# A softplus written with a biased logarithm, and the last weight splits moved from GpSimd to VectorE

## The chip, the cores and the metric

The program runs on one core of one Trainium2 chip. A core has a matrix engine (TensorE, PE in the profile; its weight loads are shown apart as PEld), VectorE (DVE), ScalarE (ACT), GpSimd (POOL) and a queue engine that issues DMAs (SyncE, SP). The metric is the device time of one execution in microseconds (us), as a median over runs.

## The reference, cut to what matters

```python
x = attention(q, k, v)                     # 1152 rows of 512
x = mixture_of_experts(x, ...)             # top 2 of 8 experts, weights w1, w2
h = x @ w_in                               # 1152 x 2048
g = np.maximum(h, 0.0) + np.log1p(np.exp(-np.abs(h)))
return (g @ w_out).astype(np.float32)      # 1152 x 512
```

The change touches only the last three lines, the feed-forward part: the function g (softplus) and the preparation of its weights. Everything is float32 and is kept close to float32 accuracy: each operand of a product is split into a high part in a rounded format and a low part (operand minus high part), and each product is made of three matmuls, high by high, high by low and low by high.

## The kernel before, in words

Attention and routing fill the first part of the span, the experts the middle, and the feed-forward part runs from about 459 us to the end. There the 1152 rows lie in four groups of 2, 3, 2 and 2 tiles of 128 rows (`CH`), and the 2048 hidden columns in 16 blocks of 128. A step n handles one group and one block: 64 steps, n = 0 to 63, and three more in which only the rest of the second product is left. The first 16 steps belong to group 0, with 256 columns in an instruction.

In step n the program issues, in this order: `act2(n-1)` on VectorE; at some steps a part of the next rows' combination (`scale0` on ScalarE and `combine` on VectorE at steps 3, 7, 11, ...; a transpose on TensorE with its two copies, tiles `xh` and `xl`, at steps 6, 10, 14, ..., and behind it two gathers, `ygather`, on GpSimd); `ff1_(n)`, the first product, 12 matmuls into the PSUM tile `ph`, then Abs and Exp on ScalarE; `act3(n-1)`, the high part `gh` of the softplus on ScalarE; `act1(n)`; the low part `gl` of step n-1 on VectorE; `split_lo`; `split_hi`; and `ff2_(n-3)`, the second product of the step three before, six matmuls for a group of two tiles, of which the third and the sixth read `gl`.

The weights come as 80 chunks of 128 by 1024 numbers, in four buffers `wraw`. `split_hi` makes a chunk's high part on ScalarE; the low part is put in a list and done by the next `split_lo` as one subtraction, behind which the load of the chunk four further on is issued by SP. The engine of that subtraction is picked once per chunk in line 169. When the feed-forward part begins, chunks 71 to 79 are still to be split, nine in all; `split_hi` takes them at steps 0 to 8, so that their low parts come at steps 1 to 9.

Each engine works its instructions strictly in the order in which the program issues them, and waits for data of other engines by semaphores. No scheduler orders this part.

Of the kernel before, what the change touches and what calls it, by code (L numbers as in the profile page):

```python
# [16 lines left out]
AF = mybir.ActivationFunctionType  # L17
OP = mybir.AluOpType
# [34 lines left out]
NWA, NWB, NWC = 6, 5, 5  # L53
# [50 lines left out]
def fused_kernel(ctx: ExitStack, tc: tile.TileContext, q, k, v, w_gate, w_noise, noise, w1, w2,  # L104
                 w_in, w_out, cs_t, out):
    nc = tc.nc
# [35 lines left out]
    pools = {}  # L142
    nxt = {"load": 0, "split": 0, "order": False}

    def load_chunk():
        s = nxt["load"]
        if s >= len(chunk_src) or s >= 8 and not nxt["order"]:
            return
        nxt["load"] += 1
        t = raw.tile([128, 1024], F32, name="wraw")  # L150
        src = chunk_src[s]() if s < 8 * E else chunk_src[s]
        nc.sync.dma_start(out=t.rearrange("p (a b) -> p a b", a=4 if s < 8 * E and s % 8 < 4 else 2), in_=src)
        chunk_raw[s] = t
# [3 lines left out]
    def wtile(i):  # L157
        return (wa if i < NWA else pools["wb"]).tile([128, 2048], F32R, name=f"w{i}")

    def split_hi():  # L160
        s = nxt["split"]
        nxt["split"] += 1
        if s >= 64 + NSLOT:
            w = pools["wc"].tile([128, 2, 1024], F32R, name="wc")
        else:
            w = wtile(s % NSLOT).rearrange("p (a b) -> p a b", a=2)
        hi, lo = w[:, 0], w[:, 1]
        r = chunk_raw.pop(s)
        lo_eng = nc.gpsimd if s < NWA or "wc" in pools else nc.vector
        nc.scalar.activation(hi, r, AF.Copy)  # L170
        chunk[s] = (hi, lo)

        def second():
            lo_eng.tensor_tensor(out=lo, in0=r, in1=hi.bitcast(F32), op=OP.subtract)  # L174
            load_chunk()
        lo_q.append(second)

    def split_lo():
        while lo_q:
            lo_q.pop(0)()  # L180

    def split_chunk():
        split_hi()
        split_lo()
# [52 lines left out]
    def win_blk(kk, f):  # L237
        h, l = chunk[64 + 2 * (f // 2)]
        o = kk * 256 + (f % 2) * 128
        return h[:, o:o + 128], l[:, o:o + 128]  # L240
# [6 lines left out]
    def mm3(ps, pairs, first, last):  # L247
        n = len(pairs)
        for i, ((ah, al), (bh, bl)) in enumerate(pairs):
            nc.tensor.matmul(ps, ah, bh, start=first and i == 0, stop=False)  # L250
            nc.tensor.matmul(ps, ah, bl, start=False, stop=False)  # L251
            nc.tensor.matmul(ps, al, bh, start=False, stop=last and i == n - 1)  # L252
# [710 lines left out]
    for g in range(2 * NP_):  # L963
        p, h = divmod(g, 2)
        for u in range(6):
            n = 5 * g + (0, 1, 2, 3, 3, 4)[u]
# [6 lines left out]
        for a in range(2):  # L973
            n = 5 * g + 3 + a
# [3 lines left out]
        n = 5 * g + 5  # L978
# [4 lines left out]
    for p in range(NP_):  # L983
        n = 10 * p
# [54 lines left out]
    for i in range(NWA):  # L1039
        op(("sp", i), "ACT", 950, 100 + i, [("ld", i) if i < 4 else ("sl", i - 4), ("rope", 7)] + [("sp", i - 1)] * (i > 0) +  # L1040
           prep7 * (i >= 4) + [("XTl", 0), ("XTl", 1)] * (i == 5), split_hi)
        op(("sl", i), "POOL", 2300, 100, [("sp", i)], lambda: lo_q.pop(0)())
# [101 lines left out]
    for _ in range(8):  # L1144
        next(r1)
    split_hi()
    for f in range(4, 8):
        gemm1(0, f, pa)
# [191 lines left out]
    def ygather(i, kk):  # L1340
        nonlocal ygt
        if ygt is None:
            ygt = yg_tile().bitcast(F32)
        o = (i % 3 if kk == 0 else 3 + i % 2) * DM
        g = ygt[:, o:o + DM]
        top = (NOV + ROW0[NR - 1] + (min(i + 1, CB) if kk else 0)) * 128
        nc.gpsimd.indirect_dma_start(out=g, out_offset=None, in_=ytab[0:top, :],
                                     in_offset=bass.IndirectOffsetOnAxis(ap=yrow[:, i, kk:kk + 1], axis=0))
        YG[i, kk] = g
# [4 lines left out]
    def scale0(i):  # L1354
        a = YG[i, 0]
        nc.scalar.activation(a, a, AF.Copy, scale=wts[:, i, 0:1])

    def combine(i):
        a, c = YG.pop((i, 0)), YG.pop((i, 1))
        nc.vector.scalar_tensor_tensor(out=c, in0=c, scalar=wts[:, i, 1:2], in1=a, op0=OP.mult, op1=OP.add)  # L1360
        YG[i] = c

    def x2_T(i, ps):
        y = YG.pop(i)
        for d in range(4):
            nc.tensor.transpose(ps[:, d, :], y[:, d * 128:(d + 1) * 128], ident)
        c, o = place[i]
        if o == 0:
            x2[c] = (mx.tile([128, 4, FC], F32R, name="xh"), mx.tile([128, 4, FC], F32R, name="xl"))
        dh, dl = (t[:, :, o * 128:(o + 1) * 128] for t in x2[c])  # L1370
        nc.scalar.activation(dh, ps, AF.Copy)
        nc.vector.tensor_tensor(out=dl, in0=ps, in1=dh.bitcast(F32), op=OP.subtract)  # L1372
# [45 lines left out]
    def ff1_(c, f):  # L1418
        w = CH[c] * 128
        ps = psh.tile([128, FC], F32, name="ph")[:, :w]  # L1420
        xh, xl = x2[c]
        mm3(ps, [(win_blk(kk, f), (xh[:, kk, :w], xl[:, kk, :w])) for kk in range(4)], True, True)
        a = ff.tile([128, FC], F32, name="fa")[:, :w]
        l = ff.tile([128, FC], F32, name="fl")[:, :w]
        u = ff.tile([128, FC], F32, name="fu")[:, :w]
        HS[c, f] = (ps, a, l, u)
        nc.scalar.activation(a, ps, AF.Abs)  # L1427
        nc.scalar.activation(a, a, AF.Exp, scale=-1.0)  # L1428

    def act1(c, f):  # L1430
        ps, a, l, u = HS[c, f]
        nc.vector.tensor_scalar(u, a, 1.0, None, op0=OP.add)  # L1432
        nc.vector.scalar_tensor_tensor(out=a, in0=u, scalar=1.0, in1=a, op0=OP.subtract, op1=OP.subtract)
        return lambda: nc.scalar.activation(l, u, AF.Ln)

    def act2(c, f):
        ps, a, l, u = HS[c, f]
        nc.vector.scalar_tensor_tensor(out=l, in0=ps, scalar=0.0, in1=l, op0=OP.max, op1=OP.add)
        nc.vector.tensor_tensor(out=l, in0=l, in1=a, op=OP.subtract)

    def act3(c, f):
        ps, a, l, u = HS.pop((c, f))
        gh = ff.tile([128, FC], F32R, name="gh", bufs=FL + 1)[:, :CH[c] * 128]
        gl = ff.tile([128, FC], F32R, name="gl", bufs=FL + 1)[:, :CH[c] * 128]
        nc.scalar.activation(gh, l, AF.Copy)
        G[c, f] = (gh, gl)
        return lambda: nc.vector.tensor_tensor(out=gl, in0=l, in1=gh.bitcast(F32), op=OP.subtract)

    def ff2_(c, f, o):
        gh, gl = G[c, f]  # L1450
        if f == 0:
            ACC[c, o] = pso.tile([128, DM], F32, name="po")
        cs = slice(o * 128, o * 128 + 128)
        mm3(ACC[c, o], [((gh[:, cs], gl[:, cs]), wout_blk(f))], f == 0, f == 15)
        if f == 15:
            i = place.index((c, o))
            po = ACC.pop((c, o))
            ot = ff.tile([128, DM], F32, name="ot", bufs=2)
            if i == NT - 1:
                nc.scalar.activation(ot[:, 0:DM // 2], po[:, 0:DM // 2], AF.Copy)  # L1460
                nc.vector.tensor_copy(out=ot[:, DM // 2:], in_=po[:, DM // 2:])
            elif o % 2:
                nc.scalar.activation(ot, po, AF.Copy)
            else:
                nc.vector.tensor_copy(out=ot, in_=po)
            for t, r0, nr, p0, p1, base in tok_maps:
                if t <= i < t + nr:
                    nc.sync.dma_start(out=ap(out, (base + i - t) * DM, [[nr * DM, p1 - p0], [1, DM]]),
                                      in_=ot[p0:p1, :])
# [6 lines left out]
    seq = [(c, f) for c in range(len(CH)) for f in range(16)]  # L1476
# [7 lines left out]
    for n in range(len(seq) + FL):  # L1484
        if 1 <= n <= len(seq):
            act2(*seq[n - 1])
        for i, u in extra.pop(n, []):
            if u == 0:
                scale0(i)
                combine(i)  # L1490
            else:
                x2_T(i, psh.tile([128, 4, 128], F32, name="px", bufs=1))
                if i + 2 < NT:
                    ygather(i + 2, 0)
                    ygather(i + 2, 1)
        if n < len(seq):
            ff1_(*seq[n])
        sub = act3(*seq[n - 1]) if 1 <= n <= len(seq) else None
        if n < len(seq):
            act1(*seq[n])()  # L1500
        if sub:
            sub()
        split_lo()
        if nxt["split"] < len(chunk_src):
            split_hi()
        if n >= FL:
            c, f = seq[n - FL]
            for o in range(CH[c]):
                ff2_(c, f, o)
# [38 lines left out]
```

## Time and the profile before

| what | us |
|---|---|
| median of 3 runs (lowest, highest) | 684.37 (683.69, 684.41) |
| profiled execution, its own time | 683.52 |
| its span, first to last instruction | 681.7 |
| busy in the span: PE, PEld | 633.8, 566.9 |
| busy in the span: DVE, ACT, POOL | 515.1, 430.9, 249.3 |

The span is what the trace shows; the 1.8 us between it and the execution's own time lie around the program. The clock that TensorE was granted is full in all 40 slices of the page.

### The profile page before, as it was taken

Reading aid. Unit: us, or ns where it says so; the run is one execution under the profiler, and the core shown is the slowest. Engines: PE = TensorE matmul, PEld = TensorE weight load, DVE = VectorE, ACT = ScalarE, POOL = GpSimd, SP = SyncE. Lnnn points to the kernel's source line nnn. Section 1 sums busy time; section 2 is a strip of 40 time slices with the busy share of each in tenths; the row PEclk is TensorE's granted clock in tenths of the full one; section 3 lists DMA queues with packets and bytes.
Section 4 is the critical chain, followed back from the end, with each engine's and each line's share of the span. In section 5 each row is a group of like instructions: output and inputs, shape, how many; then the busy total and the mean of one; then the engine's idle time right before and its main releaser. Section 6 shows DMA issues by size and latency. Waiting matters only on the chain.

```text
span 681.7 us, 11588 instructions
## 1 busy us (share of the span) xinstructions
PE 633.8 (93%) x4066; PEld 566.9 (83%) x4066; DVE 515.1 (76%) x1054; ACT 430.9 (63%) x912; POOL 249.3 (37%) x250
## 2 busy tenths in 40 slices
PE   2899999889988999999999999977799999999997
PEld 2798989868987898988889798956579999899996
DVE  6889899999985658849686776837997655676665
ACT  2887888668973656747576576726565544465553
POOL 6968976762465202432323232316650100000000
PEclk9999999999999999999999999999999999999999
DMA  6318421002342959997999999764311100100000
GB/s 152 95 42 308 134 56 55 1 19 76 120 129 85 341 161 302 345 319 275 327 311 329 313 314 340 245 233 137 96 53 43 45 17 0 46 2 1 32 1 31
DMA packets 67900, 101.07 MB, mean 148 GB/s; under 512 B 11232, under 2 KB 38624, under 8 KB 67840
## 3 DMA queue, kind: packets, MB, share of 16 engines
q1 hardware_dynamic: 61552, 84.59, 38.2%
q0 software_dynamic: 3136, 10.10, 4.5%
q10 hardware_dynamic: 3152, 5.62, 2.2%
q8 instruction: 33, 0.54, 0.3%
q14 instruction: 27, 0.22, 0.1%
HBM read 76.70 MB, written 23.59 MB: 147 GB/s over the span
## 4 chain that ended last, share of the span: by engine, by line
PE 57%; DVE 4%; ACT 4%; DMA 2%; issue 0%; ACTq 0%; DVEq 0%; SPq 0%
PE p L250 9%; PE p L251 9%; PE p L252 9%; PE po L252 4%; PE po L251 4%; PE po L250 4%; PE ph L250 4%; PE ph L252 4%; PE ph L251 4%; DVE fu L1432 2%; DMA wraw<-wtab 2%; PE p L1117 2%; PE pa L1073 1%; PE p L1119 1%; DVE yg L1360 1%; ACT wc L170 1%
## 5 line engine op out<-in xcount | busy, mean ns | idle before, releaser
L219 POOL TENSOR_TENSOR dm<-dm,da 128x512 int32<-128x512 int32 x32 | 42.1, 1314 | 134.1 <-DVE da L216 61.2
L174 DVE TENSOR_TENSOR w<-wraw,w 128x1024 fp32r<-128x1024 f32 x65 | 88.6, 1374 | 1.2 <-ACT w L170 1.2
L170 ACT ACTIVATE w<-wraw 128x1024 fp32r<-128x1024 f32 x75 | 78.7, 1055 | 8.7 <-DMA wraw<-in_moe_w_dram 7.9
L251 PE MATMUL p<-xl,w 128*128 128x320 f32 (+3 forms) x256 | 77.4, 303 | 0.3 <-DVE xl L1076 0.3
L250 PE MATMUL p<-xh,w 128*128 128x320 f32 (+3 forms) x256 | 77.4, 303 | 0.0
L252 PE MATMUL p<-xh,w 128*128 128x320 f32 (+3 forms) x256 | 77.3, 302 | 0.0
L1432 DVE TENSOR_SCALAR fu<-fa 128x256 f32<-128x256 f32 (+1 forms) x64 | 31.5, 492 | 56.5 <-ACT fa L1428 56.5
L1427 ACT ACTIVATE fa<-ph 128x256 f32<-128x256 f32 (+1 forms) x64 | 26.1, 407 | 68.1 <-PE ph L252 68.1
L483 ACT ACTIVATE P<-ps,nmx 128x576 f32<-128x576 f32 (+1 forms) x80 | 59.2, 740 | 12.8 <-DVE nmx L475 11.7
L475 DVE TENSOR_REDUCE nmx<-ps 128x1 f32<-128x576 f32 (+1 forms) x80 | 60.0, 751 | 7.4 <-PE ps L462 5.6
L518 ACT ACTIVATE pth<-pt 128x512 fp32r<-128x512 f32 (+2 forms) x96 | 53.4, 569 | 9.2 <-PE pt L496 4.9
L250 PE MATMUL p<-w,hb 128*128 128x512 f32 x144 | 58.7, 407 | 0.0
L250 PE MATMUL ph<-xh,w 128*128 128x256 f32 (+1 forms) x192 | 57.2, 298 | 1.4 <-DVE xl L1372 1.4
L1093 DVE SCALAR_TENSOR_TENSOR hb<-p,hb 128x256 fp32r<-128x256 f32 (+1 forms) x104 | 31.6, 346 | 34.0 <-ACT hb L1089 32.4
L252 PE MATMUL ph<-xh,w 128*128 128x256 f32 (+1 forms) x192 | 56.7, 295 | 0.0
L251 PE MATMUL ph<-xl,w 128*128 128x256 f32 (+1 forms) x192 | 56.7, 295 | 0.0
L252 PE MATMUL p<-w,hb 128*128 128x512 f32 x144 | 56.6, 393 | 0.0
L251 PE MATMUL p<-w,hb 128*128 128x512 f32 x144 | 56.6, 393 | 0.0
L448 DVE TENSOR_TENSOR ptl<-pt,pth 128x512 fp32r<-128x512 f32 (+1 forms) x80 | 49.5, 629 | 1.7 <-ACT pth L518 1.2
L251 PEld LDWEIGHTS p<-xl,w 128*128 128x128 f32 x256 | 48.2, 188 | 0.8 <-DVE xl L1076 0.5
L250 PEld LDWEIGHTS p<-xh,w 128*128 128x128 f32 x256 | 48.2, 188 | 0.7 <-ACT xh L1075 0.2
L252 PEld LDWEIGHTS p<-xh,w 128*128 128x128 f32 x256 | 48.2, 188 | 0.0
(291 smaller groups left out, 1882.2 us busy)
## 6 DMA issues: line engine op xcount, KB each, us to landing
wraw<-in_moe_w_dram SPq DMA_DIRECT2D x64, 512.0 KB
x<-in_moe_w_in_dram SPq DMA_DIRECT2D x16, 512.0 KB
x<-in_moe_w_out_dram SPq DMA_DIRECT2D x16, 512.0 KB
wtab<-dm SPq DMA_DIRECT2D x32, 256.0 KB
wraw<-wtab SPq DMA_DIRECT2D x16, 512.0 KB
ytab<-y ACTq DMA_DIRECT2D x18, 256.0 KB
ytab<-zrow SPq DMA_DIRECT2D x1, 4096.0 KB
w<-in_v_dram SPq DMA_DIRECT2D x8, 256.0 KB
```

Source lines behind the costliest of these rows:

```text
L170: nc.scalar.activation(hi, r, AF.Copy)
L174: lo_eng.tensor_tensor(out=lo, in0=r, in1=hi.bitcast(F32), op=OP.subtract)
L219: nc.gpsimd.tensor_tensor(out=m, in0=m, in1=ai, op=OP.add)
L250: nc.tensor.matmul(ps, ah, bh, start=first and i == 0, stop=False)
L251: nc.tensor.matmul(ps, ah, bl, start=False, stop=False)
L252: nc.tensor.matmul(ps, al, bh, start=False, stop=last and i == n - 1)
L448: nc.vector.tensor_tensor(out=dl, in0=x, in1=dh.bitcast(F32), op=OP.subtract)
L475: nc.vector.tensor_reduce(out=nmx[p0:p1], in_=stS[n][p0:p1, :, :HN], axis=AX.XY, op=OP.max, negate=True)
L483: nc.scalar.activation(Pt[p0:p1, 0:S].rearrange("p (a c) -> p a c", a=2), ps[p0:p1, :, :HN], AF.Exp, bias=nmx[p0:p1], scale=1.0, accum_out ...
L518: nc.scalar.activation(*evac.pop(("T", g, u)), AF.Copy)
L1093: nc.vector.scalar_tensor_tensor(out=o, in0=ps[:, c], scalar=0.0, in1=hh[:, c].bitcast(F32), op0=OP.max, op1=OP.subtract)
L1432: nc.vector.tensor_scalar(u, a, 1.0, None, op0=OP.add)
```

## The change

Three edits, all in the feed-forward part. The logarithm log(1 + a), with a = Exp(-|h|), is taken on ScalarE from a with a bias of one, directly behind the Exp, where before VectorE made u = 1 + a and ScalarE took the logarithm of u. VectorE makes the rounding correction from u = (1 + a) - 1 as a - u, with a two-operation instruction and a subtraction, where before it was (u - 1) - a; `act2` adds it now. And the low parts of the last nine chunks, 71 to 79, are made by VectorE.

```diff
         r = chunk_raw.pop(s)
-        lo_eng = nc.gpsimd if s < NWA or "wc" in pools else nc.vector
+        lo_eng = nc.gpsimd if s < NWA else nc.vector
         nc.scalar.activation(hi, r, AF.Copy)
...
         nc.scalar.activation(a, ps, AF.Abs)
         nc.scalar.activation(a, a, AF.Exp, scale=-1.0)
+        nc.scalar.activation(l, a, AF.Ln, bias=1.0)
 
     def act1(c, f):
+
         ps, a, l, u = HS[c, f]
-        nc.vector.tensor_scalar(u, a, 1.0, None, op0=OP.add)
-        nc.vector.scalar_tensor_tensor(out=a, in0=u, scalar=1.0, in1=a, op0=OP.subtract, op1=OP.subtract)
-        return lambda: nc.scalar.activation(l, u, AF.Ln)
+        nc.vector.tensor_scalar(u, a, 1.0, 1.0, op0=OP.add, op1=OP.subtract)
+        nc.vector.tensor_tensor(out=a, in0=a, in1=u, op=OP.subtract)
 
     def act2(c, f):
         ps, a, l, u = HS[c, f]
         nc.vector.scalar_tensor_tensor(out=l, in0=ps, scalar=0.0, in1=l, op0=OP.max, op1=OP.add)
-        nc.vector.tensor_tensor(out=l, in0=l, in1=a, op=OP.subtract)
+        nc.vector.tensor_tensor(out=l, in0=l, in1=a, op=OP.add)
...
         if n < len(seq):
-            act1(*seq[n])()
+            act1(*seq[n])
```

VectorE, from step 1 of the feed-forward part, before: `fu` and `fa` are the tiles u and a, `fl` the logarithm and then the softplus.

```order
L1432 TENSOR_SCALAR fu<-fa 128x256
L1433 SCALAR_TENSOR_TENSOR fa<-fu,fa 128x256
L1447 TENSOR_TENSOR gl<-fl,gh 128x256
L1438 SCALAR_TENSOR_TENSOR fl<-ph,fl 128x256
L1439 TENSOR_TENSOR fl<-fl,fa 128x256
```

The same place in the changed kernel, from step 1 to the beginning of step 2, where `w_6040` is the tile of chunk 71.

```order
L1434 TENSOR_SCALAR fu<-fa 128x256
L1435 TENSOR_TENSOR fa<-fa,fu 128x256
L1448 TENSOR_TENSOR gl<-fl,gh 128x256
L174 TENSOR_TENSOR w_6040<-wraw,w_6040 128x1024
L1439 SCALAR_TENSOR_TENSOR fl<-ph,fl 128x256
L1440 TENSOR_TENSOR fl<-fl,fa 128x256
```

A subtraction of 1024 columns has come in between the low part `gl` and the next `act2`, in each of steps 1 to 9; the five others stand where they stood.

ScalarE from the split of chunk 71 on, step 0 to step 1, before:

```order
L170 ACTIVATE w_6040<-wraw 128x1024
L1427 ACTIVATE fa<-ph 128x256
L1428 ACTIVATE fa<-fa 128x256
L1445 ACTIVATE gh<-fl 128x256
L1434 ACTIVATE fl<-fu 128x256
L170 ACTIVATE w_6072<-wraw 128x1024
```

and in the changed kernel:

```order
L170 ACTIVATE w_6040<-wraw 128x1024
L1427 ACTIVATE fa<-ph 128x256
L1428 ACTIVATE fa<-fa 128x256
L1429 ACTIVATE fl<-fa 128x256
L1446 ACTIVATE gh<-fl 128x256
L170 ACTIVATE w_6072<-wraw 128x1024
```

The logarithm stands ahead of `gh` now, reads `fa` and no longer `fu`, and the split of the next chunk stands behind `gh`.

GpSimd, the end of its work, as a difference of the two programs:

```order
-L1347 DMA yg<-ytab,yrow 128x512 x4
-L174 TENSOR_TENSOR w_6040<-wraw,w_6040 128x1024
-L174 TENSOR_TENSOR w_6072<-wraw,w_6072 128x1024
-L174 TENSOR_TENSOR w_6104<-wraw,w_6104 128x1024
-L174 TENSOR_TENSOR w_6138<-wraw,w_6138 128x1024
-L174 TENSOR_TENSOR wc<-wraw,wc 128x1024
-L1347 DMA yg<-ytab,yrow 128x512 x2
-L174 TENSOR_TENSOR wc<-wraw,wc 128x1024 x4
-L1347 DMA yg<-ytab,yrow 128x512 x8
+L1347 DMA yg<-ytab,yrow 128x512 x14
```

GpSimd is left with the gathers alone, in the order in which they stood.

## Rows read from the trace of the kernel before

**Rows 1.** Windows: start:end, length, busy (x instructions) of PE, PEld, DVE, ACT, POOL; clock, DMA.
```profile
459.00:505.00 46.00, 35.44 (x223) 29.65 (x224) 37.63 (x60) 27.40 (x60) 29.89 (x17) 1.00 0.32 98
505.00:532.00 27.00, 27.00 (x153) 24.73 (x152) 20.54 (x49) 16.65 (x40) 1.95 (x2) 1.00 0.16 50
532.00:600.00 68.00, 68.00 (x371) 61.30 (x370) 42.61 (x94) 34.87 (x77) 2.84 (x3) 1.00 0.08 24
```

**Rows 2.** Waits, 459 to 505 us: in total, times, longest.
```profile
PE po L252 <- DVE gl L1447: 10.2, 9, 1.9
```

**Rows 3.** Timeline of PE: start, length, work, and idle before it.
```profile
467.23 0.50 PE L252 MATMUL po<-w,gl 128*128 128x512 f32 x1 [1.44 <-DVE gl L1447]
...
476.91 0.60 PE L1366 MATMUL px<-ident,yg 128*128 128x128 f32 x4
477.27 0.36 PE L250 MATMUL ph<-xh,w 128*128 128x256 f32 x1
...
501.60 0.50 PE L252 MATMUL po<-w,gl 128*128 128x512 f32 x1 [0.93 <-DVE gl L1447]
...
667.56 0.28 PE L250 MATMUL ph<-xh,wc 128*128 128x256 f32 x1
...
670.38 0.28 PE L250 MATMUL ph<-xh,wc 128*128 128x256 f32 x1
```

**Rows 4.** Timeline of DVE.
```profile
464.50 1.88 DVE L1432 TENSOR_SCALAR fu<-fa 128x256 f32<-128x256 f32 x1 [0.78 <-ACT fa L1428]
...
466.76 0.42 DVE L1447 TENSOR_TENSOR gl<-fl,gh 128x256 fp32r<-128x256 f32 x1
...
502.26 0.68 DVE L1372 TENSOR_TENSOR xl<-px,xh 128x512 fp32r<-128x512 f32 x1
502.86 0.42 DVE L1432 TENSOR_SCALAR fu<-fa 128x256 f32<-128x256 f32 x1
...
504.79 0.74 DVE L1360 SCALAR_TENSOR_TENSOR yg<-yg,wts 128x512 f32<-128x512 f32 x1
505.45 0.29 DVE L1432 TENSOR_SCALAR fu<-fa 128x256 f32<-128x256 f32 x1
505.77 0.43 DVE L1433 SCALAR_TENSOR_TENSOR fa<-fu,fa 128x256 f32<-128x256 f32 x1
506.11 0.42 DVE L1447 TENSOR_TENSOR gl<-fl,gh 128x256 fp32r<-128x256 f32 x1
506.45 0.42 DVE L1438 SCALAR_TENSOR_TENSOR fl<-ph,fl 128x256 f32<-128x256 f32 x1
506.90 0.43 DVE L1439 TENSOR_TENSOR fl<-fl,fa 128x256 f32<-128x256 f32 x1
507.24 0.28 DVE L1432 TENSOR_SCALAR fu<-fa 128x256 f32<-128x256 f32 x1
```

**Rows 5.** Timeline of POOL.
```profile
463.83 2.40 POOL L174 TENSOR_TENSOR w<-wraw,w 128x1024 fp32r<-128x1024 f32 x1 [0.20 <-ACT w L170]
...
502.02 1.14 POOL L1347 DMA_INDIRECT yg<-ytab,yrow  x1 [0.31 <-issue]
```

**Rows 6.** Timeline of ACT in step 1 and at the beginning of step 2.
```profile
463.65 0.36 ACT L1427 ACTIVATE fa<-ph 128x256 f32<-128x256 f32 x1
464.05 0.42 ACT L1428 ACTIVATE fa<-fa 128x256 f32<-128x256 f32 x1
...
466.41 0.42 ACT L1434 ACTIVATE fl<-fu 128x256 f32<-128x256 f32 x1 [1.64 <-DVE fu L1432]
466.74 1.04 ACT L170 ACTIVATE w<-wraw 128x1024 fp32r<-128x1024 f32 x1
467.68 0.37 ACT L1427 ACTIVATE fa<-ph 128x256 f32<-128x256 f32 x1
```

**Rows 7.** Line 174 on DVE: ns of one, smallest, median and largest; where.
```profile
L174 DVE TENSOR_TENSOR w<-wraw,w x65: 1206/1216/2260, 211.6 to 445.7; 128x1024 fp32r<-128x1024 f32 x65
```

**Rows 8.** Groups of DVE, shapes apart: busy us, mean ns of one, idle before.
```profile
L683 DVE TENSOR_SCALAR c<-e 128x40 f32<-128x40 f32 x1 | 0.2, 184 | 0.3 <-ACT e L679 0.3
...
L805 DVE TENSOR_SCALAR keep<-sw 128x9 f32<-128x9 f32 x1 | 0.2, 165 | 0.0
```

## The prediction, written before the changed kernel was run

> **What bounds the kernel now.** I read the windows first. From 459 to 505 us, where the feed-forward part begins, TensorE is busy for 35.44 of 46.00 us; behind that its two windows are full, 27.00 of 27.00 and 68.00 of 68.00 us, at a granted clock of 1.00 throughout [rows 1]. So time is to be had only in that first stretch, and a gain there is kept: the rest is work of TensorE that follows on. The waits say what TensorE waited for there: nine times for `gl`, the low part of the softplus, 10.2 us in all [rows 2].
>
> The timeline of TensorE gives the true size of it. The first of the nine waits ends at 467.23 and the last at 501.60, eight steps and 34.37 us later [rows 3]. A step of two tiles takes 2.82 us where nothing waits (667.56 to 670.38), and one transpose group 0.36 (476.91 to 477.27), of which two lie between [rows 3]. At full rate the eight steps would take 8 x 2.82 + 0.72 = 23.28 us. So 11.09 us are lost between the two, and with the first wait's own 1.44 us [rows 3] 12.5 us: the most that any change of this stretch can give.
>
> Why `gl` is late stands in the timelines of the other engines. VectorE's TENSOR_SCALAR of line 1432 lasts 1.88 us at 464.50, against 0.29 at 505.45 [rows 4]. The long one lies under a subtraction of a chunk's low part on GpSimd, 463.83 to 466.23 [rows 5], and ends 0.15 us behind it. ScalarE's logarithm waits for its result, 1.64 us [rows 6]. A loop goes round in each step: TENSOR_SCALAR to logarithm 1.91 us (464.50 to 466.41) [rows 4, 6], logarithm to chunk split 0.33, split to the next Abs 0.94, Abs to Exp 0.40 [rows 6], Exp to the next TENSOR_SCALAR 0.45 (464.05 to 464.50) [rows 4, 6]; sum 4.03 us. The split releases the next subtraction on GpSimd, so that the next TENSOR_SCALAR meets it again. Eight turns are 32.2 us; the rest of the 34.37 is the combination's work at three of the steps.
>
> **The change part by part.** *GpSimd's nine subtractions go* (nine chunks, front section). With them goes the long TENSOR_SCALAR; behind the last of them it stands at 0.29 us (505.45) [rows 4].
>
> *VectorE takes nine subtractions.* Line 174 costs 1.216 us there as a median [rows 7]; as the next instruction does not read its result, some 0.08 us overlap, as 0.42 us instructions follow each other at 0.34 (506.11 to 506.45) [rows 4]: 1.14 us. The other five of a step follow at 0.32, 0.34, 0.34, 0.45 and 0.34 (505.45 to 507.24) [rows 4], 1.79 us. A step of VectorE with a split is thus 2.93 us; `combine` adds 0.66 (504.79 to 505.45) at steps 3 and 7, `xl` 0.60 (502.26 to 502.86) at step 6 [rows 4].
>
> *The correction's new forms.* A subtraction of two tensors in the place of line 1433 has the shape of line 1447, 0.42 us [rows 4]: no difference. A TENSOR_SCALAR with two operations and 256 columns is not in the trace. Two small ones are: 165 ns at 9 columns and 184 at 40 [rows 8], 0.61 ns a column, which makes 184 + 216 x 0.61 = 316 ns; from above it is bounded by a two-tensor instruction's 0.42 us, from below by the 0.29 of before [rows 4]. I take 0.29, since 0.61 a column is much nearer to (0.29 - 0.165) / 247 = 0.51 than to the two-tensor (0.42 - 0.165) / 247 = 1.03.
>
> *The biased logarithm.* It no longer waits for VectorE. ScalarE's chain from the end of `act2(n-1)` to the next step's TENSOR_SCALAR is now `gh` 0.33 (taken as the logarithm's), split 0.94, Abs 0.40, Exp 0.45 [rows 6]: 2.12 us, under VectorE's 2.93. So ScalarE is 0.8 us ahead in these steps, and both VectorE's new wait (the subtraction of line 1435 overwrites `fa`, so it comes behind the logarithm) and `gh` (behind the logarithm too) are covered by it. Without that cover, where VectorE keeps pace with TensorE, the subtraction starts 0.1 us later (logarithm's end 0.84 behind the Exp's start, TENSOR_SCALAR's at 0.77, and the signal). That is the case in steps 10 to 63, where VectorE needs 1.79 of 2.82 us and `gl` is wanted two steps later; uncovered it would be 0.1 x 54 = 5 us.
>
> *The sum.* In step 0 the logarithm starts without VectorE's reply, so that the split, Abs and Exp of step 1 come 0.45 us earlier, Exp at 463.60. TENSOR_SCALAR at 464.05, the subtraction behind the logarithm at 464.48, `gl(0)` at 464.82, the chunk at 465.16, `act2(1)` at 466.30, TENSOR_SCALAR at 467.10, `gl(1)` at 467.76. From there VectorE's step counts: `gl(2)` starts at 467.76 + 2.93 + 0.66 = 471.35, then 474.28, 477.21, 480.74 (with `xl`), 484.33 (with `combine`), 487.26 and `gl(8)` at 490.19. TensorE can use each 0.47 us later (466.76 to 467.23) [rows 3, 4]. It would want `gl(0)` at 467.23 - 1.44 = 465.79 and has it; `gl(1)` too; it waits for `gl(2)`, 471.82 against 471.43. From 471.82 it comes to `gl(4)` at 477.82 unhindered (two steps and a transpose group), waits for `gl(5)` until 481.21 and for `gl(6)` until 484.80, and goes on with a transpose group at full rate: `gl(8)` at 484.80 + 5.64 + 0.36 = 490.80, where VectorE has it at 490.66. Before, this matmul stood at 501.60 [rows 3]: **10.8 us less**.
>
> *GpSimd's gathers* now stand first in its queue and start as soon as a transpose is done; four of them fall in the stretch. A TENSOR_SCALAR under a gather took 0.42 us (502.86; gather 502.02 to 503.16) [rows 4, 5], 0.13 more than alone: four times that is 0.5 us off. Here the Trainium skill, "SBUF — State Buffer", section "SBUF: two separate sides", says more: VectorE and GpSimd share a port pair that is locked for a whole instruction, and the loser blocks fully. The rows agree for the long TENSOR_SCALAR; for the gather it is a rival below, as the 0.42 us one can't tell a short hold from a late start.
>
> 10.8 - 0.5 = 10.3 us. From the profiled execution's 683.52 that leaves 673.2; the median of the runs shown is 684.37, 0.85 higher, and would make it 674.1. I say **673.6**.
>
> Moved loads: the load of the fourth chunk on is issued behind each subtraction, and that chunk's split comes three steps later, 3 x 2.93 = 8.8 us where it was 3 x 4.03 = 12.1. The DMA engines are busy 0.32 of the stretch [rows 1], so I cost it at nothing.
>
> **The rivals.** (a) *VectorE's step is heavier than 2.93 us*: TENSOR_SCALAR at 0.42 (+0.13), no overlap behind the chunk (+0.08), the wait for the logarithm not covered (+0.1), together 0.31 us, 8 x 0.31 = 2.5 us: 676.1, and half of it 674.9. For it speaks that three engines hand over to each other; against it the 0.8 us by which ScalarE is ahead.
> (b) *Each gather holds VectorE for its whole length.* At most one TENSOR_SCALAR can meet a gather, since a pair takes about one step; 1.14 us [rows 5] for two pairs are 2.3 us instead of the 0.5, 675.4. The section named above would have it so.
> (c) *TensorE runs at its full rate*: VectorE's step comes in at under 2.7 us and all of the 12.5 us come free: 671.1. Against it stands the sum of six measured intervals.
> (d) *No change*: the loop is held by something else that takes 4 us, the loads: if a load took the 8.8 us, the splits would wait and the step would stay near 4.03. Gain under 1.4 us. Against it: 0.32 of the DMA engines' time.
> (e) *Slower: the long TENSOR_SCALAR is its own*, not GpSimd's, and stays 1.88 us with the chunk's subtraction on top. Then VectorE's step is 2.93 + 1.59 = 4.52, and eight are 36.2 + 1.92 for the three extras = 38.1 us against 34.37: 3.7 us slower, 687.2. It decides from 1.42 us on, where eight steps take 34.37. Against it: 0.29 at 505.45, the first steps without a subtraction on GpSimd [rows 4].
>
> **How the numbers follow.** Forecast, between 672 and 674.5: 0.60. (a) 0.17, (b) 0.07, (c) 0.09, (d) 0.04, (e) 0.03. The range of 8 in 10 takes in (c) and most of (a) and (b): 671.0 to 676.2. A measurement of this kernel tells 0.2%, 1.4 us, from no change; all but (d) and (e) are faster by more: 0.93, 0.04, 0.03.
>
> **What would show it.** Right: in the first 45 us of the feed-forward part no TENSOR_SCALAR over 0.5 us, TensorE's waits for `gl` down from nine and 10.2 us to about three and 2 us, VectorE nearly without idle time from step 2 to step 9, the logarithm without a wait, and everything behind `gl(8)` shifted by 10 to 11 us. Wrong: a long instruction of VectorE beside a gather (b), waits for `gl` at each step (a), a split that waits for its load (d).

## The result, and the profile after

The changed kernel takes 675.98 us (675.34 to 676.37, 4 runs) against 684.39 (683.69 to 684.82) beside it: ratio 0.9862 [0.9843 to 0.9881], which is 9.4 us less (8.1 to 10.7). The two medians by themselves lie 8.4 us apart, inside that interval. The changed kernel's profiled execution took 676.09 us over a span of 674.3.

The windows over the two stretches of [rows 1], same columns:

```profile
459.00:505.00 46.00, 44.29 (x274) 37.95 (x273) 39.01 (x87) 34.77 (x75) 11.19 (x10) 0.96 0.38 116
505.00:532.00 27.00, 27.00 (x143) 24.72 (x142) 19.05 (x42) 14.85 (x31) 0.94 (x1) 1.00 0.08 29
```

TensorE, busy for 35.44 us of the first stretch before, is busy for 44.29; GpSimd, 29.89 before, for 11.19. What TensorE still waits for stands in the waits of this stretch (those on VectorE's softplus work, into `ph` and `po`; total, times, longest):

```profile
PEld ph L250 <- DVE fl L1439: 2.1, 5, 0.7
...
PEld po L252 <- DVE gl L1448: 1.6, 4, 0.5
...
PE ph L250 <- DVE fl L1439: 0.3, 1, 0.3
```

All but one of these waits are idle times of the weight load ahead of a matmul. Before, the weight loads waited for `gl` in this stretch as follows (the 10.2 us of [rows 2] are those of the matmuls):

```profile
PEld po L252 <- DVE gl L1447: 14.1, 9, 2.3
```

The second line after is this old reason, the low part `gl`, 1.6 us where it was 14.1; no row of the matmuls themselves names `gl` any more. The first line is new: a matmul into `ph` that waits for `act2` (line 1439) to have read that tile of PSUM.

VectorE's timeline, from the TENSOR_SCALAR of one step to that of the next, and the low parts of steps 9 and 10 (before: [rows 4]):

```profile
475.92 0.28 DVE L1434 TENSOR_SCALAR fu<-fa 128x256 f32<-128x256 f32 x1
476.31 0.43 DVE L1435 TENSOR_TENSOR fa<-fa,fu 128x256 f32<-128x256 f32 x1
476.65 0.42 DVE L1448 TENSOR_TENSOR gl<-fl,gh 128x256 fp32r<-128x256 f32 x1
476.99 1.22 DVE L174 TENSOR_TENSOR w<-wraw,w 128x1024 fp32r<-128x1024 f32 x1
478.12 0.42 DVE L1439 SCALAR_TENSOR_TENSOR fl<-ph,fl 128x256 f32<-128x256 f32 x1
478.57 0.42 DVE L1440 TENSOR_TENSOR fl<-fl,fa 128x256 f32<-128x256 f32 x1
478.92 0.29 DVE L1434 TENSOR_SCALAR fu<-fa 128x256 f32<-128x256 f32 x1
...
492.89 0.42 DVE L1448 TENSOR_TENSOR gl<-fl,gh 128x256 fp32r<-128x256 f32 x1
...
496.49 0.42 DVE L1448 TENSOR_TENSOR gl<-fl,gh 128x256 fp32r<-128x256 f32 x1
```

There is no idle time in brackets: VectorE is the engine that sets the pace here, with 3.00 us a step (475.92 to 478.92). TENSOR_SCALAR lasts 0.28, over the whole kernel at most 0.364, as the instructions of its line show (ns of one, smallest, median, largest; first and last start):

```profile
L1434 DVE TENSOR_SCALAR fu<-fa x64: 280/295/364, 463.9 to 665.4; 128x256 f32<-128x256 f32 x48, 128x384 f32<-128x384 f32 x16
```

How much the part gained is read between its first and its last matmul. TensorE's timeline after, with three of the matmuls that read `gl` between, for `gl(0)`, `gl(8)` and `gl(9)`:

```profile
460.63 0.39 PE L250 MATMUL ph<-xh,w 128*128 128x256 f32 x1 [1.41 <-DVE xl L1372]
...
468.38 0.39 PE L252 MATMUL po<-w,gl 128*128 128x512 f32 x1
...
493.84 0.39 PE L252 MATMUL po<-w,gl 128*128 128x512 f32 x1
...
496.96 0.50 PE L252 MATMUL po<-w,gl 128*128 128x512 f32 x1
...
669.62 0.39 PE L252 MATMUL po<-wc,gl 128*128 128x512 f32 x1
```

and the first and the last of them before:

```profile
459.36 0.39 PE L250 MATMUL ph<-xh,w 128*128 128x256 f32 x1 [1.41 <-DVE xl L1372]
...
677.05 0.39 PE L252 MATMUL po<-wc,gl 128*128 128x512 f32 x1
```

The part took 217.69 us and takes 208.99, that is 8.70 less. It begins 1.27 us later after, though nothing ahead of it was changed.

One thing differs that the change did not ask for. Windows of 5 us, after; the third figure from the end is the granted clock:

```profile
455.00:460.00 5.00, 2.70 (x14) 1.86 (x14) 2.07 (x4) 1.79 (x3) 0.39 (x1) 1.00 0.32 106
460.00:465.00 5.00, 4.37 (x24) 4.38 (x25) 1.58 (x4) 1.97 (x4) 3.03 (x4) 0.66 0.34 92
```

Behind a stretch in which TensorE was busy for 2.70 of 5 us its clock fell to the lower of its two levels, 1.2 of 2.4 GHz, in the first steps of the part: 0.66 on the mean of the window, and 24 matmuls in these 5 us. At 218 to 223 us the clock was at 0.66 once already. The profiled execution of before had full clock in both places.

### The profile page after: what moved, and what is told of

Same layout as the page of the kernel before. It is cut to its first block, busy times and chain, and to the rows that moved or that the text cites. A ratio compares the mean times of both kernels' runs of the same rounds, so it can differ in the third digit from the quotient of the medians.

```text
span 674.3 us, 11714 instructions
## 1 busy us (share of the span) xinstructions
PE 636.9 (94%) x4066; PEld 569.7 (84%) x4066; DVE 509.9 (76%) x1063; ACT 432.8 (64%) x912; POOL 228.4 (34%) x241
## 4 chain that ended last, share of the span: by engine, by line
PE 62%; issue 2%; DMA 2%; DVE 1%; ACT 0%; POOL 0%; POOLq 0%; DVEq 0%
PE p L250 10%; PE p L251 10%; PE p L252 10%; PE ph L250 5%; PE po L252 5%; PE ph L251 5%; PE ph L252 5%; PE po L251 5%; PE po L250 5%; PE p L1117 2%; PE p L1119 2%; PE pa L1073 1%; DMA yg<-ytab,yrow 1%; DMA ytab<-y 1%; PE px L1366 0%
## 5 line engine op out<-in xcount | busy, mean ns | idle before, releaser
L174 DVE TENSOR_TENSOR w<-wraw,w 128x1024 fp32r<-128x1024 f32 x69 | 93.8, 1370 | 1.2 <-ACT w L170 1.2
L250 PE MATMUL ph<-xh,w 128*128 128x256 f32 (+1 forms) x192 | 58.4, 304 | 1.7 <-DVE xl L1372 1.4
L252 PE MATMUL ph<-xh,w 128*128 128x256 f32 (+1 forms) x192 | 57.4, 299 | 0.0
L1434 DVE TENSOR_SCALAR fu<-fa 128x256 f32<-128x256 f32 (+1 forms) x64 | 19.8, 309 | 47.2 <-ACT fa L1428 46.9
L1347 POOL DMA_INDIRECT yg<-ytab,yrow x18 | 18.9, 1048 | 92.5 <-PE px L1366 71.6
L250 PEld LDWEIGHTS p<-xh,w 128*128 128x128 f32 x256 | 48.2, 188 | 0.6 <-ACT xh L1075 0.2
```

## The experiments

The theory (A): GpSimd's subtractions held VectorE's TENSOR_SCALAR, and moving them is the whole gain; the logarithm's edit only shortens a chain that is covered. The rivals: the logarithm's edit brings the gain by itself; and of what is missing from the forecast, the clock, the gathers, a tile that two engines share, or the crowding of the first steps.

**One half of the change alone.** The low parts on VectorE, with the old logarithm (against before):

```diff
-        lo_eng = nc.gpsimd if s < NWA or "wc" in pools else nc.vector
+        lo_eng = nc.gpsimd if s < NWA else nc.vector
```

> Only the engine of the nine low parts is changed, the logarithm stays behind VectorE's 1 + a. Theory A (GpSimd's subtractions hold VectorE's TENSOR_SCALAR, and moving them away is the whole gain): TENSOR_SCALAR 0.29 us in every step, VectorE's step 2.93 us, the loop through ScalarE 2.44 us and hidden under it; 676 us, as the whole change, within 0.7 us. Rival B (the gain comes from taking the logarithm out of the loop between VectorE and ScalarE): the loop stays, less than half of the gain, 681 us or more.

676.17 us, ratio 0.9849 [0.9827 to 0.9872]: the gain of the whole change. Its VectorE, from the timeline:

```profile
471.00 0.29 DVE L1432 TENSOR_SCALAR fu<-fa 128x256 f32<-128x256 f32 x1
471.32 0.43 DVE L1433 SCALAR_TENSOR_TENSOR fa<-fu,fa 128x256 f32<-128x256 f32 x1
...
474.59 0.29 DVE L1432 TENSOR_SCALAR fu<-fa 128x256 f32<-128x256 f32 x1
...
477.52 0.29 DVE L1432 TENSOR_SCALAR fu<-fa 128x256 f32<-128x256 f32 x1
```

TENSOR_SCALAR is short, the next instruction follows 0.32 us behind it, not 0.39 as after the change, and a step takes 2.93 us (474.59 to 477.52).

**The other half.** The new logarithm, with the low parts on GpSimd (against after, that line turned back):

```diff
-        lo_eng = nc.gpsimd if s < NWA else nc.vector
+        lo_eng = nc.gpsimd if s < NWA or "wc" in pools else nc.vector
```

> Only the logarithm and the correction are changed, the nine low parts stay on GpSimd. Theory A in its strict form (the move is needed): TENSOR_SCALAR still waits 1.5 us and more for GpSimd in each of these steps, and the time stays at 684 us within 1 us. Rival B: the next chunk's split no longer waits for VectorE, GpSimd's 2.40 us run beside, and the step falls to about 2.8 to 3.4 us although TENSOR_SCALAR still meets GpSimd: 675 to 680 us. In that case either edit would open the loop by itself.

685.83 us, ratio 0.9999 [0.9984 to 1.0013]: no change. VectorE's timeline:

```profile
466.17 1.97 DVE L1434 TENSOR_SCALAR fu<-fa 128x256 f32<-128x256 f32 x1 [0.44 <-ACT fa L1428]
468.24 2.37 DVE L1435 TENSOR_TENSOR fa<-fa,fu 128x256 f32<-128x256 f32 x1
...
470.87 0.41 DVE L1439 SCALAR_TENSOR_TENSOR fl<-ph,fl 128x256 f32<-128x256 f32 x1
```

and GpSimd's at that place:

```profile
465.49 4.84 POOL L174 TENSOR_TENSOR w<-wraw,w 128x1024 fp32r<-128x1024 f32 x2 [1.26 <-ACT w L170]
```

Both long instructions lie under two subtractions on GpSimd, 465.49 to 470.33; the second ends 0.28 us behind them. The logarithm no longer waits for TENSOR_SCALAR, but everything behind it on VectorE does, and TensorE's weight loads still wait for `gl`: 9.6 us in three waits, the longest 4.3, where before it was 14.1 us in nine. Around two of the long waits TensorE's clock is at its lower level for a part of the time (0.66 on the mean of 470 to 475 us, 0.59 of 490 to 495), and over the whole run it is 0.981 to 0.995 against 0.987 to 1.000 for the kernel before. Whether this edit would be worth something by itself at an equal clock is therefore not shown. What is shown is that the move alone brings the whole gain and the logarithm's edit alone none, so (A) stands.

**A tile of its own for the correction.** In the changed kernel the subtraction writes a - u over a, which the logarithm reads on ScalarE; here it writes over u (against after):

```diff
-        nc.vector.tensor_tensor(out=a, in0=a, in1=u, op=OP.subtract)
+        nc.vector.tensor_tensor(out=u, in0=a, in1=u, op=OP.subtract)
...
-        nc.vector.tensor_tensor(out=l, in0=l, in1=a, op=OP.add)
+        nc.vector.tensor_tensor(out=l, in0=l, in1=u, op=OP.add)
```

> The whole change, but the correction a - u is written into u and no longer over a, so that VectorE's subtraction needn't wait for the logarithm. If the 0.07 us by which each step of VectorE was longer than forecast (TENSOR_SCALAR to subtraction 0.39 instead of 0.32) is that second wait: 0.32 again, a step with a chunk 2.93 instead of 3.00, time 675.4 (0.6 us less than the whole change). If it is the two-operation form of TENSOR_SCALAR: 0.39 stays, 676.0.

675.33 us, ratio 0.9855 [0.9831 to 0.9879], not to be told from the change. The step is what the forecast had:

```profile
472.00 0.29 DVE L1434 TENSOR_SCALAR fu<-fa 128x256 f32<-128x256 f32 x1
472.32 0.43 DVE L1435 TENSOR_TENSOR fu<-fa,fu 128x256 f32<-128x256 f32 x1
...
474.93 0.28 DVE L1434 TENSOR_SCALAR fu<-fa 128x256 f32<-128x256 f32 x1
```

0.32 us between the two, and 2.93 for a step (472.00 to 474.93). In the changed kernel a separate semaphore instruction stands in VectorE's queue ahead of each of the 64 subtractions. Its ns (smallest, median, largest), and what VectorE waited for ahead of these subtractions (us in total, times):

```profile
L1435 DVEq EVENT_SEMAPHORE  x64: 21/21/300, 463.9 to 665.8; - x64
...
ACT fl L1429: 7.8, 46
```

Here there is no such instruction. In steps 2 to 14 of the changed kernel the logarithm is done in time and 0.38 to 0.40 us lie between the two instructions; from about step 15 on the subtraction does wait for it, 0.44 to 0.56 us behind TENSOR_SCALAR in most steps. That costs nothing: TensorE is busy for 68.00 of 68.00 us from 532 to 600 us. This execution had no stretch of lower clock in the feed-forward part, which took 207.76 us.

**The splits spread out.** By the kernel, TensorE reads the first of the nine chunks in step 8 (chunk 72) and the last in step 17, so the nine splits need not stand in nine neighbouring steps (against after):

```diff
-        if nxt["split"] < len(chunk_src):
+        if nxt["split"] < len(chunk_src) and n in SPLITS:    # SPLITS = (0, 2, 4, 5, 7, 8, 10, 11, 12)
```

> The whole change, but the nine chunks are split at steps 0, 2, 4, 5, 7, 8, 10, 11, 12 instead of 0 to 8. If what is left of TensorE's loss in the stretch (2.5 us) is VectorE's step of 3.00 against TensorE's 2.82: VectorE keeps up, TensorE's waits for the low part and for the free PSUM tile nearly go, 674.0 us. If it is something else (transposes, loads, clock): 676 us.

676.57 us, ratio 0.9864 [0.9841 to 0.9887]: nothing gained. TensorE's weight loads show a new wait, in step 14:

```profile
502.56 0.19 PEld L252 LDWEIGHTS ph<-xh,wc 128*128 128x128 f32 x1 [1.77 <-DVE wc L174]
```

A chunk (78, split at step 11 here) was now split too late for the step that reads it, which costs 1.77 us; the waits for `gl` fell to 0.5 us. This execution also had the lower clock at the beginning of the part (209.25 us for the part).

**The changed kernel once more**, beside the next three.

> The changed kernel unaltered, timed again with more runs of both. Theory: the change is worth 10 to 10.8 us in the stretch, and the 8.4 us of the first comparison were four runs against four in which short stretches of halved clock fell unevenly: 9.5 to 10.8 us less than the kernel before, ratio 0.9845 to 0.986. Rival: 8.4 us is its true worth, ratio 0.9877, and 1.5 to 2 us of the forecast are lost for good.

676.81 us against 686.26, ratio 0.9862 [0.9842 to 0.9882], that is 9.45 us less, at the lower edge of what was expected. Its part took 209.89 us with the lower clock at about 460 to 467.

**Own tile and a spread with earlier ends**: the edit of the own tile, and `SPLITS = (0, 1, 3, 4, 5, 7, 8, 9, 11)`.

> The correction in its own tile, and the chunks split at steps 0, 1, 3, 4, 5, 7, 8, 9, 11, so that no low part falls on the steps with a combination (3, 7) and the ones that TensorE needs first come four steps ahead. If what is left of TensorE's waits is VectorE's step with a chunk being longer than TensorE's 2.82 us: the waits for the low part and for the PSUM tile of the stretch fall from about 3.7 us of weight-load idle time to under 1 us, TensorE's time from the first matmul of the feed-forward part to the last at full clock from 207.5 to about 205.5 us, 1.5 to 2 us less than the whole change. If VectorE isn't what is left: no difference.

674.47 us, ratio 0.9826 [0.9807 to 0.9846]. The new wait is gone, and of the waits of weight loads for `gl` these are the two longest:

```profile
476.30 0.19 PEld L252 LDWEIGHTS po<-w,gl 128*128 128x128 f32 x1 [0.23 <-DVE gl L1448]
...
488.14 0.19 PEld L252 LDWEIGHTS po<-w,gl 128*128 128x128 f32 x1 [0.30 <-DVE gl L1448]
```

The part took 206.85 us although it began at the lower clock. Against the own tile alone the intervals overlap; the trace carries the verdict.

**Work for TensorE ahead of the part.** The own tile, and 38 transposes of the identity into a PSUM tile that nobody reads, put into the idle times before the first feed-forward matmul (against the own tile):

```diff
+    def fill(n):
+        ps = ps1.tile([128, CAP], F32, name="p1")
+        for _ in range(n):
+            nc.tensor.transpose(ps[:, 0:128], ident, ident)
...
+    fill(20)   # ahead of x2_T(0)
+    fill(6)    # ahead of x2_T(1)
+    fill(12)   # behind x2_T(1)
```

> The correction in its own tile, and 38 idle transposes (20, 6 and 12, of the identity into a PSUM tile that nobody reads) where TensorE waits for the last combination before the feed-forward part; no result depends on them. If the halved clock at the beginning of the feed-forward part (3.3 us at half, 1.5 us lost) follows from TensorE's idle time just before: no such stretch near 460 us in this kernel's profile, and about 1 us less on the median, as most runs have it. If it has nothing to do with that idle time: the dip stays, and the time is that of the own-tile kernel or up to 0.5 us more for the transposes.

675.05 us, ratio 0.9842 [0.9825 to 0.9858]; mean granted clock 0.997 in each of five runs. The same windows as above:

```profile
455.00:460.00 5.00, 4.46 (x32) 3.69 (x32) 2.13 (x3) 1.79 (x3) 0.20 (x1) 1.00 0.28 102
460.00:465.00 5.00, 5.00 (x45) 5.00 (x44) 2.20 (x6) 3.55 (x9) 3.65 (x4) 1.00 0.52 136
```

With TensorE busy for 4.46 of the 5 us ahead, the clock stays at 1.00, and 45 matmuls are done where after had 24. The part takes 207.75 us, as with the own tile alone in an execution that had the full clock by itself, with 2.69 us busy of the same 5. So one trace can't show that the transposes did it. Of the ten traces without them, eight have the lower clock at the beginning of the part; of the two with them (this one and the next), none. That speaks for the transposes without proving it.

**All three together**: own tile, the second spread, the idle transposes.

> Own tile, spread chunks and idle transposes together: if the three add up, about 3 us less than the whole change, 672.5 us on a chip where that takes 675.5; ratio to the kernel before about 0.981.

673.03 us (672.35 to 674.96), ratio 0.9812 [0.9797 to 0.9826], clear of the changed kernel's 0.9842 to 0.9882 beside it: 3.8 us under the change and some 13 under before, the fastest of all. The part takes 206.07 us.

**Before once more**, for its clock.

> The kernel before, unaltered, for another trace of it. If a stretch of halved clock falls on the beginning of its feed-forward part, as in three of the changed kernel's kind: the first product is late by about 1.5 us, but TensorE waits for the low part there anyway, so that the time from the first matmul of the part to the last grows by under 1 us from its 217.7 us, where the changed kernel's grows by 1.5. That would take 0.5 to 1 us of the forecast gain in such runs. If it grows by 1.5 us too, the dips cancel between the kernels.

One execution, 686.22 us. Its windows:

```profile
460.00:465.00 5.00, 4.05 (x21) 4.05 (x22) 0.94 (x2) 0.97 (x3) 2.84 (x3) 0.66 0.34 88
490.00:495.00 5.00, 3.39 (x12) 3.01 (x13) 4.48 (x6) 2.97 (x6) 2.97 (x2) 0.68 0.05 16
```

So the kernel before loses the clock there too, in this execution and not in the other, and here once more at 490 to 495 us, among its own waits for `gl`. Its first matmul of the part stands at 460.95, as late as in the changed kernel; the part took 218.77 us.

**GpSimd busy on a scratch tile.** The changed kernel, and for each of the nine chunks two subtractions of 512 columns on GpSimd into a tile that nobody reads; to make room, the output has one buffer instead of two (against after):

```diff
+            if "wc" in pools:
+                gt = pools["gt"].tile([128, 512], F32, name="gt")
+                for o in (0, 512):
+                    nc.gpsimd.tensor_tensor(out=gt, in0=r[:, o:o + 512], in1=hi[:, o:o + 512].bitcast(F32),
+                                            op=OP.subtract)
...
-            ot = ff.tile([128, DM], F32, name="ot", bufs=2)
+            ot = ff.tile([128, DM], F32, name="ot", bufs=1)
```

> The whole change, and GpSimd makes the nine low parts too, in two halves each into a scratch tile that nobody reads (for the room of it the output tile has one buffer instead of two). VectorE waits for none of it. Theory A (VectorE and GpSimd shut each other out while both work on SBUF, without any data between them): long instructions of VectorE come back, 1 us and more each, and TensorE waits for the low part again: 682 us or more. Rival (the long instruction came from the order of the data, chunk split, subtraction, load): no long instruction, 676 us within 1 us.

697.45 us, ratio 1.0173 [1.0122 to 1.0223]. The single output buffer has a share in that time (ScalarE waits 11.1 us for it, VectorE 5.1), so only the durations are used. VectorE:

```profile
468.01 1.41 DVE L1441 TENSOR_TENSOR fa<-fa,fu 128x256 f32<-128x256 f32 x1
...
469.35 1.48 DVE L1454 TENSOR_TENSOR gl<-fl,gh 128x256 fp32r<-128x256 f32 x1
470.75 2.31 DVE L179 TENSOR_TENSOR w<-wraw,w 128x1024 fp32r<-128x1024 f32 x1
...
475.97 0.42 DVE L1445 SCALAR_TENSOR_TENSOR fl<-ph,fl 128x256 f32<-128x256 f32 x1
476.42 1.07 DVE L1446 TENSOR_TENSOR fl<-fl,fa 128x256 f32<-128x256 f32 x1
```

under this work of GpSimd:

```profile
466.39 5.58 POOL L177 TENSOR_TENSOR gt<-wraw,w 128x512 f32<-128x512 f32 x4 [1.41 <-ACT w L170]
475.38 3.26 POOL L177 TENSOR_TENSOR gt<-wraw,w 128x512 f32<-128x512 f32 x2 [3.41 <-issue]
```

No instruction of VectorE reads the scratch tile or waits for it, and still those with two operands in SBUF are lengthened, from 0.42 to 1.07, 1.41 and 1.48 and from 1.22 to 2.31 us. The one at 475.97, which reads one operand in PSUM and one in SBUF, lies under GpSimd's work too and takes its usual 0.42. Over all 64 of it:

```profile
L1445 DVE SCALAR_TENSOR_TENSOR fl<-ph,fl x64: 410/418/553, 465.7 to 686.0; 128x256 f32<-128x256 f32 x48, 128x384 f32<-128x384 f32 x16
```

it is never lengthened (0.553 is its form of 384 columns), though four of the 64 lie under a subtraction on GpSimd. So the hold comes from GpSimd's access alone, not from data; TENSOR_SCALAR is held here too (up to 1.39).

## Why the prediction was right, and where its sum was off

The measured 675.98 lies in the range, though only 0.2 under its upper end, and 2.4 above the forecast; it is outside the 672 to 674.5 that had the largest chance. Of the sum's 10.3 us, 9.4 came by the ratio and 8.4 by the medians; in the trace of the part, 8.70 of the 10.8 ahead of the term for the gathers. The mechanism was right, and the sum was too large by about 2 us in the part. Step by step:

- **The mechanism held.** No TENSOR_SCALAR over 0.364 us; the two halves of the change show that moving the subtractions brings all of it, and the logarithm's edit nothing that can be measured. Rival (e), the long TENSOR_SCALAR being its own, is excluded by the same rows, and (d) by a step of 3.00 instead of 4.03 us; no split waited for a load in this stretch. Of the signs named, one did not come: the matmul of `gl(8)` was to shift by 10 to 11 us and shifted by 7.8 (501.60 to 493.84), or 9.0 counted from the first matmul of the part.
- **VectorE's step, 2.93 forecast, 3.00 measured.** The moved subtraction cost 1.22 with 0.09 overlapped (476.99 to 478.12, where 1.14 was taken), and the two-operation TENSOR_SCALAR 0.28, where 0.29 was taken. What was missed is that the subtraction that overwrites a waits for two engines: 0.39 us behind TENSOR_SCALAR (475.92 to 476.31) where 0.32 was taken. The wait was looked at and costed at nothing, since ScalarE is ahead. In steps 2 to 9 the logarithm is indeed ready, but the wait for it costs 0.07 us a step. The kernels with a tile of its own, and with the old logarithm, are both back at 2.93. That is rival (a), at a fifth of its price.
- **The sum ended a step too early.** It stopped at `gl(8)` and took full rate from there. But step 9 splits the last chunk and step 10 carries an `xl`: by the sum's own figures `gl(9)` starts at 490.19 + 2.93 + 0.60 = 493.72, is usable at 494.19, and TensorE is there at 490.80 + 2.82 = 493.62. 0.57 us of the 10.8 were never there. In the trace this matmul does wait: the one at 496.96, 0.47 behind the low part of 496.49.
- **VectorE ran 1.5 us later than the sum.** The matmul of `gl(9)` stands 496.96 - 460.63 = 36.33 us behind the start of the part; the sum gives 494.19 - 459.36 = 34.83. Of this, 7 x 0.07 = 0.5 from `gl(1)` to `gl(8)` is the step above. The other 1.0 is there by `gl(1)` (470.00 - 460.63 = 9.37 against 8.40): 0.6 since the first TENSOR_SCALAR starts 3.27 us behind the first matmul (463.90) instead of 2.67 (462.03 in the trace of before), its matmuls running at the lower clock, and 0.4 in step 1 and its subtraction. 10.8 - 0.57 - 1.5 = 8.7, which is what the part gained. The execution with its own tile and the full clock had `gl(1)` 8.48 behind its start and took 207.76 us; 217.69 less 10.8 - 0.57 is 207.46.
- **The gathers, 0.5 forecast: not there**, nor rival (b). No TENSOR_SCALAR of this trace was longer than 0.364. That taking off this 0.5 brought the forecast nearer to the measured time is luck. It is the gather that gives way, in GpSimd's timeline after:

```profile
476.03 0.99 POOL L1347 DMA_INDIRECT yg<-ytab,yrow  x1 [10.28 <-PE px L1366]
477.33 1.69 POOL L1347 DMA_INDIRECT yg<-ytab,yrow  x1 [0.30 <-DVE gl L1448]
...
490.57 1.69 POOL L1347 DMA_INDIRECT yg<-ytab,yrow  x1 [0.30 <-DVE gl L1448]
```

  The second begins under the long subtraction of line 174 (476.99 to 478.21) and takes 1.69 us, ending 0.81 behind it; the first, beside three short instructions of VectorE, takes 0.99, and none of those is lengthened. Nobody waits for either. The 0.42 us at 502.86 from which the 0.5 was taken [rows 4] did not come again in this trace. It did in others: 0.42 at 505.52 in the second execution of before, 0.435 at 464.25 with the idle transposes, both 0.6 to 0.9 us behind the beginning of a gather. Others that began as late in a gather took 0.29. So a gather can hold a TENSOR_SCALAR for some 0.15 us, the short hold of the sum; what decides it stays open.
- **Between trace and median.** The part gained 8.70 between the two profiled executions but began 1.27 us later. That comes from the stretch of lower clock at 218 to 223 us, which this execution of before did not have: the same matmul stands at 210.48 before and 210.01 after, and a later one at 224.55 and 225.75. Against the other execution of before, which lost its clock at the same two places and at a third, the part gained 218.77 - 208.99 = 9.8. The 9.4 by the ratio lies between. That the clock moves between executions of one kernel was not in the prediction: its bounds rested on one trace at 1.00.
- **What TensorE still loses.** From the matmul at 468.38 to the one at 496.96 are 28.58 us for nine steps and two transpose groups; at full rate 9 x 2.82 + 0.72 = 26.10. About 2.5 us are left. All three additions together bring the part from 208.99 to 206.07 us: 1.24 of that come with the tile of its own in an execution at full clock (207.75), 1.68 with the spread. Rival (c) needed a step under 2.7 us, which the change alone does not reach.
- **Two prices of rivals.** The forecast of 673.6 with its 10.3 us starts from 683.9. From there (c), 12.5 us less, is 671.4 and not 671.1, and (e), 3.7 us more, is 687.6 and not 687.2. It changes no verdict.

Here the Trainium skill, "SBUF — State Buffer", section "SBUF: two separate sides", says that a VectorE instruction in a two-port mode, or with two SBUF inputs beside a GpSimd operation that reads SBUF, and the GpSimd operation exclude each other for a whole instruction. The runs agree: 0.29 to 1.97, and 0.42 to 2.37 or 1.48, for the former, 0.42 unchanged for the instruction with one input from PSUM (475.97 in the run with the scratch tile). The same rule gives the pair to the one that starts first: the two gathers of 1.69 us each began 0.34 behind a subtraction with two SBUF inputs (476.99 and 490.23), which fits; but no gather held an instruction of VectorE for its whole 0.95 us, which the rule would have, as rival (b) did, if that whole row were one hold.

## What to carry to other kernels

A long duration of a short VectorE instruction can be a wait that no wait row names: lay GpSimd's timeline beside it, and price moving GpSimd's work against the whole loop that the instruction holds up (nine subtractions of 1.14 us cost VectorE about 10 us, and the kernel became 9.4 us faster). Carry such a sum on until the first step at which the engine that waits is late no more, and do not write a result over a tile that another engine still reads. Where added work is not needed at once, spread it over more steps, but only as far as each piece is still ready for its user: one spread gained nothing through a single wait of 1.77 us, the next, with earlier ends, brought 1.68 us of the part.

## What was not expected of the hardware

- The granted clock changes from one execution of the same kernel to the next. In the kernel before TensorE kept the full clock at 460 us in one execution, after 2.89 us busy of 5, and fell to the lower level for a little over 3 us in another, after 2.69; the kernel with its own tile kept it after 2.69. With 38 idle transposes ahead of that place it stayed at 1.00 in both profiled executions (4.46 and 3.04 us busy of 5). For the other runs of these kernels only the mean clock is known.
- A wait for a second engine can stand in the queue as an instruction of its own, here of 21 ns at the median. Even where the logarithm was already there, in steps 2 to 9, the chain was 0.07 us longer with it.
- An instruction of VectorE that is held by GpSimd counts as busy: 4.84 us for a TENSOR_SCALAR in the kernel with the logarithm's edit alone, with no row in the waits.
